# One load of x in place of two, on SP's queue and re-formed by VectorE, in a decode kernel

## The chip, the cores and the metric

The kernel runs on one core of one Trainium2 chip. The metric is the device time of one execution in microseconds (us). For the kernel before, three runs gave 407.74, 407.78 and 407.82 us; the median is 407.78. The profile is of one more execution, which took 407.74 us.

## The reference, cut to what matters

One token's x (1024 numbers) is normalised, then two blocks are computed from the normalised row and added to x: an attention block A over a cache of 65,536 positions with 4 key/value heads and 32 query heads, and a mixer/MLP block B.

```python
def _layernorm(x, axis=-1, eps=1e-5):
    m = jnp.mean(x, axis=axis, keepdims=True)
    v = jnp.var(x, axis=axis, keepdims=True)
    return (x - m) / jnp.sqrt(v + eps)

def _A_ref(x, k_cache, v_cache, wq, wo):
    q = (x @ wq) as 32 heads of 128
    scores = q . k * (128 ** -0.5)        # each key head serves 8 query heads
    o = softmax(scores) . v
    return o @ wo

def _B_ref(x, w1, w2, w3, w4):
    h = _gelu(_layernorm(x) @ w1)
    hs = (h, shifted along a sequence of length one, so zeros) @ w2
    x1 = x + hs
    return x1 + _gelu(_layernorm(x1) @ w3) @ w4

xn = _layernorm(A_x)
return A_x + _A_ref(xn, ...) + _B_ref(xn, ...)
```

All inputs are bfloat16. The cache is 2 x 64 MB, the weights together 35.7 MB, x is 2 KB.

## The kernel before, in words

**What is loaded.** One list, `order` (lines 585 to 598), names all large loads in the order in which they are used: four of wq, one of w1, one of w2, four of w3, then keys and values in turn, with wo in between and w4 last. Most are 2 MB, as 16 KB on each of 128 partitions (w3: 14 KB). All are issued by SP on its own DMA queue (`load`, line 276; q1 on the page) into nine slots of `slots_sb` that are used in rotation. `issue_to(NS - 1)` (line 614) issues the first nine; after the code of item i has been laid out, `issue_to(i + 9)` (line 641) issues the load that reuses its slot, and SP waits for the last reader of that slot first. w4's last two slots are loaded in pieces (`load_pieces`, line 284).

**How the order is made.** `_Q` collects each engine's instructions in program order, and `_op`, `_grp` and `_dma` add waits from what each tile was last written and read by (`_B`). An engine works through its list in order; a wait holds up all that is behind it on that engine. All waits of SP for its slots are at line 48.

**Constants.** GpSimd fills constants until about 8 us (lines 343 to 366), among them `ones_f` and the masks; `b_const` marks their end. TensorE's first three small matmuls (lines 374 to 376) wait for it.

**x.** It is loaded twice, by two DMAs that ACT issues (its queue is q10 on the page). `xP_bf` (line 368) is x on 128 partitions, 8 numbers each; `xr_bf` (line 370) is x as four rows of 256 numbers on partitions 0, 32, 64 and 96, into a tile that VectorE has set to zero (line 369). Both count on one semaphore, and the cast of `xP_bf` to float32 `xP` (line 372) waits for both.

**The norm and its users.** `layer_norm` (from line 391) reduces `xP` on VectorE, sums over partitions with a TensorE matmul against ones (lines 393 and 401), takes the power on GpSimd (line 405) and leaves `xn_bf`. Then VectorE makes `accr` from `xr_bf`, `ln_s` and `xr_bf` again (lines 601 and 603): x plus its normalised form in four rows, to which the results of all products are added at the end (line 642). `rows_mv` (line 411) multiplies a vector with a loaded slab: its matmuls (line 417) leave the result as four rows, one for each quarter of the columns. `use_wq` does so for wq, two slabs' rows at a time, into two PSUM banks.

**From rows to partitions.** `to_p` (line 420) brings such four rows to 128 partitions: one VectorE transpose of 32x32 blocks (line 421) into `X32[:, 1, ...]`, the second half of the tile that the key transposes also use, from which every 32nd column is then read. w1, w2, wq and w3 use it for their results.

**Attention.** For each key load VectorE makes four transposes (line 499) and TensorE multiplies (line 506); VectorE takes the maximum (line 511), ACT the exponential (line 530); TensorE transposes the weights (line 539) and multiplies with the value loads (line 552). `wo` and `w4` products follow at line 417, and SP stores the result (line 643).

Of the kernel before, what the change touches and what calls it, by code (L numbers as in the profile page):

```python
# [6 lines left out]
BF = mybir.dt.bfloat16  # L7
F32 = mybir.dt.float32
ACTF = mybir.ActivationFunctionType
ALU = mybir.AluOpType  # L10
# [64 lines left out]
def _deps(q, reads, writes):  # L75
    for b in reads:
        for s, v in b.w.items():
            q.wait((s, v))
    for b in writes:
        for s, v in b.w.items():  # L80
            q.wait((s, v))
        for s, v in b.r.items():
            q.wait((s, v))


def _done(ev, reads, writes, partial=False):
    for b in reads:
        b.add_read(ev)
    for b in writes:
        if partial:  # L90
            b.add_write(ev)
        else:
            b.set_write(ev)


def _op(q, fn, reads=(), writes=(), partial=False):
    _deps(q, reads, writes)
    ev = q.op(fn, True)
    _done(ev, reads, writes, partial)
    return ev  # L100
# [17 lines left out]
def _dma(q, chan, fn, reads=(), writes=(), partial=False):  # L118
    _deps(q, reads, writes)
    chan.n += 1  # L120
    ev = q.dma(fn, chan.sem, 16 * chan.n)
    _done(ev, reads, writes, partial)
    return ev
# [10 lines left out]
def bass_parallel_sum__gqa_block_cached__mixer_s_mlp__decode_kernel(  # L134
# [14 lines left out]
    P = 128  # L149
# [6 lines left out]
    R = D // P  # L156
# [10 lines left out]
    RW = D // 4  # L167
# [7 lines left out]
    with ExitStack() as es:  # L175
# [3 lines left out]
        def sb(name, shape, dt):  # L179
            return E(nc.sbuf_tensor(name, shape, dt))  # L180
# [4 lines left out]
        def sem(name):  # L185
            return E(nc.semaphore(name))
# [12 lines left out]
        neghalf = sb("neghalf", [P, 1], F32)  # L199
        permWE = sb("permWE", [P, 4, P], BF)  # L200
        maskA = sb("maskA", [P, 4, G], F32)
        xP_bf = sb("xP_bf", [P, R], BF)
        xP = sb("xP", [P, R], F32)
        xn = sb("xn", [P, R], F32)
        xn_bf = sb("xn_bf", [P, R + 32], BF)
# [5 lines left out]
        ln_s = sb("ln_s", [P, 8], F32)  # L211
# [21 lines left out]
        cb_o = sb("cb_o", [P, R], F32)  # L233
        oP_bf = sb("oP_bf", [P, HKV * R + 32], BF)
        xr_bf = sb("xr_bf", [P, RW], BF)
        accr = sb("accr", [P, RW], F32)
        g_bf = sb("g_bf", [P, R + 32], BF)
        ge_x = sb("ge_x", [P, NT], F32)
# [14 lines left out]
        q_dve = _Q("dve", sem("c_dve"))  # L253
        q_act = _Q("act", sem("c_act"))
        q_pool = _Q("pool", sem("c_pool"))
        q_sp = _Q("sp", None)
        ch_x = _DmaChan(sem("d_x"))
        ch_out = _DmaChan(sem("d_out"))
        slots = [_Slot(slots_sb[:, i, :], _B("slot%d" % i), _DmaChan(sem("d_s%d" % i))) for i in range(NS)]

        b_const = _B(); b_xb = _B(); b_x = _B(); b_xn = _B(); b_xn2 = _B(); b_x1 = _B(); b_xn3 = _B()
        b_ln = _B(); b_qT = _B(); b_Y = _B(); b_misc = _B(); b_ge = _B()
        b_X = [[_B() for _ in range(4)] for _ in range(2)]
        b_S = [_B() for _ in range(NCH)]
# [3 lines left out]
        b_Bst = _B(); b_brun = [_B(), _B()]; b_dd = _B(); b_ff = _B()  # L268
        b_p = _B(); b_pT = [_B(), _B()]; b_lcol = [_B(), _B()]; b_lsum = _B(); b_Lacc = _B(); b_O = _B()
        b_cb = _B(); b_oP = [_B() for _ in range(HKV)]  # L270
        b_xr = _B(); b_accr = _B(); b_h1 = _B(); b_gh = _B(); b_fin = _B()


        n_load = [0]
# [1 line left out]
        def load(src, width=SLOT):  # L276
            sl = slots[n_load[0] % NS]
            n_load[0] += 1
            view = sl.view[:, 0:width]
            _dma(q_sp, sl.chan, lambda e, view=view, src=src: e.dma_start(out=view, in_=src), writes=[sl.buf])  # L280
            return view, sl.buf
# [83 lines left out]
                                                          compare_op=ALU.not_equal, fill=1.0, base=-16 * j, channel_multiplier=1))  # L365
        b_const.set_write(ev)

        _dma(q_act, ch_x, lambda e: e.dma_start(out=xP_bf[:, :], in_=A_x[0, 0, :].rearrange("(p r) -> p r", p=P)), writes=[b_xb])
        _op(q_dve, lambda e: e.memset(xr_bf[:], 0.0), writes=[b_xr])
        _dma(q_act, ch_x, lambda e: e.dma_start(out=xr_bf[0:P:32, :], in_=A_x[0, 0, :].rearrange("(j m) -> j m", j=4)), writes=[b_xr])  # L370
        b_xb.add_write((ch_x.sem, 16 * ch_x.n))
        _op(q_dve, lambda e: e.tensor_copy(xP[:], xP_bf[:]), reads=[b_xb], writes=[b_x])

        _op(q_pe, lambda e: e.matmul(M1_ps[:, 0:P], selGT_bf[:, :], selGT_bf[:, :], start=True, stop=True), reads=[b_const], writes=[b_M1])
        _op(q_pe, lambda e: e.matmul(M1_ps[:, P:P + 8], selGT_bf[:, :], ident_bf[0:8, 0:8], start=True, stop=True), reads=[b_const], writes=[b_M1], partial=True)
# [13 lines left out]
        X32 = X[:].bitcast(F32)  # L389

        def layer_norm(src, b_src, dst_f, dst_bf, b_dst, c0):
            _op(q_dve, lambda e: e.reduce_sum(ln_s[:, 0:1], src[:], axis=AX.X), reads=[b_src], writes=[b_ln])
            _op(q_pe, lambda e: e.matmul(M0_ps[:, c0:c0 + 1], ones_f[:, :], ln_s[:, 0:1], start=True, stop=True),  # L393
                reads=[b_ln, b_const], writes=[b_M0])
            _op(q_dve, lambda e: e.tensor_scalar(out=ln_s[:, 1:2], in0=M0_ps[:, c0:c0 + 1], scalar1=-1.0 / D, scalar2=None, op0=ALU.mult),
                reads=[b_M0], writes=[b_ln])
            _op(q_dve, lambda e: e.tensor_scalar(out=ln_xc[:], in0=src[:], scalar1=ln_s[:, 1:2], scalar2=None, op0=ALU.add),
                reads=[b_src, b_ln], writes=[b_ln])
            _op(q_dve, lambda e: e.tensor_tensor(out=ln_sq[:], in0=ln_xc[:], in1=ln_xc[:], op=ALU.mult), reads=[b_ln], writes=[b_ln])
            _op(q_dve, lambda e: e.reduce_sum(ln_s[:, 2:3], ln_sq[:], axis=AX.X), reads=[b_ln], writes=[b_ln])  # L400
            _op(q_pe, lambda e: e.matmul(M0_ps[:, c0 + 1:c0 + 2], ones_f[:, :], ln_s[:, 2:3], start=True, stop=True),  # L401
                reads=[b_ln, b_const], writes=[b_M0])
            _op(q_dve, lambda e: e.tensor_scalar(out=ln_s[:, 3:4], in0=M0_ps[:, c0 + 1:c0 + 2], scalar1=1.0 / D, scalar2=EPS,
                                                 op0=ALU.mult, op1=ALU.add), reads=[b_M0], writes=[b_ln])
            _op(q_pool, lambda e: e.tensor_tensor(out=ln_s[:, 4:5], in0=ln_s[:, 3:4], in1=neghalf[:, 0:1], op=ALU.pow),
                reads=[b_ln, b_const], writes=[b_ln])
            _op(q_dve, lambda e: e.tensor_scalar(out=dst_f[:], in0=ln_xc[:], scalar1=ln_s[:, 4:5], scalar2=None, op0=ALU.mult),
                reads=[b_ln], writes=[b_dst])
            _op(q_dve, lambda e: e.tensor_copy(dst_bf[:, 0:R], dst_f[:]), reads=[b_dst, b_const], writes=[b_dst])
# [10 lines left out]
        def to_p(src, c0, n, b_src):  # L420
            _op(q_dve, lambda e: e.transpose(out=X32[:, 1, c0:c0 + 32 * n], in_=src), reads=b_src, writes=[b_X[1][0]], partial=c0 > 0)  # L421
# [168 lines left out]
        for n in range(NK):  # L590
# [6 lines left out]
        order.append(("wo", HKV - 1))  # L597
        order += [("w4", i) for i in range((F + 1023) // 1024)]

        layer_norm(xP, b_x, xn, xn_bf, b_xn, 0)  # L600
        _op(q_dve, lambda e: e.tensor_scalar(out=accr[:], in0=xr_bf[:], scalar1=ln_s[:, 1:2], scalar2=ln_s[:, 4:5], op0=ALU.add, op1=ALU.mult),
            reads=[b_xr, b_ln], writes=[b_accr])
        _op(q_dve, lambda e: e.tensor_tensor(out=accr[:], in0=accr[:], in1=xr_bf[:], op=ALU.add), reads=[b_xr, b_accr], writes=[b_accr])
        loaders = {"wq": load_wq, "w1": lambda: load(w1_v[:, 0:SLOT]), "w2": lambda: load(w2_v[:, 0:SLOT]), "w3": load_w3, "wo": load_wo, "w4": load_w4,
                   "k": load_k, "v": load_v}

        issued = []

        def issue_to(i):
            while len(issued) <= i and len(issued) < len(order):  # L610
                it = order[len(issued)]
                issued.append(loaders[it[0]](*it[1:]))

        issue_to(NS - 1)
        for i, it in enumerate(order):
            kind, args = it[0], it[1:]
            ld = issued[i]
            if kind == "wq":
                if args[0] == 3:
                    late_consts()  # L620
                    layer_norm(xn, b_xn, xn2, xn2_bf, b_xn2, 2)
                use_wq(args[0], ld)
            elif kind == "k":
                g, ch = args
                use_k(g, ch, ld)
                if ch == 0 and g > 0:
                    transpose_p(g - 1)
                if ch == NCH - 1:
                    finish_group(g)
            elif kind == "v":  # L630
                g, a = args
                if g == NG - 1 and a == 0:
                    transpose_p(g)
                use_v(g, a, ld)
                if a == NA - 1:
                    flash(g)
                    if g % GPH == GPH - 1:
                        combine(g // GPH)
            else:
                dict(w1=use_w1, w2=use_w2, w3=use_w3, wo=use_wo, w4=use_w4)[kind](*args, ld)  # L640
            issue_to(i + NS)
# [37 lines left out]
```

## Time and profile before

| | |
|---|---|
| runs of the kernel before, median (lowest to highest) | 407.78 us (407.74 to 407.82) |
| the profiled execution | 407.74 us |
| its span, from the first to the last instruction | 406.0 us |
| mean granted TensorE clock | 0.591 of full speed |
| busy: TensorE matmul, VectorE, ACT, GpSimd | 169.5, 201.0, 64.9, 7.5 us |
| SP's queue q1 | 169.88 MB in 12,536 packets, 98.7% of 16 DMA engines' span |
| ACT's queue q10 (the two loads of x) | 152 packets, 0.0% |
| instruction fetches (q8 and q14) | 18 packets, 0.25 MB |
| read from HBM | 169.87 MB, 418 GB/s over the span |

Times in the profile are in us from the span's start. Engines are PE (TensorE matmul), PEld (its weight load), DVE (VectorE), ACT, POOL (GpSimd) and SP; a "q" behind the name is the engine's sequencer, which issues DMAs. L499 is line 499 of the kernel. A row of the timeline has start, duration, engine, line, operation, the tile written, the tile read, shapes and a count; in brackets stands how long the engine was idle before and what ended that. A row of the windows has the stretch, its length, each engine's busy time with the number of instructions, the granted TensorE clock, the busy share of the 16 DMA engines and the GB/s that they moved. The chain of waits follows the work that ended last back to the start. The trace also keeps each DMA packet's queue, start, duration and size; a semaphore write is a packet of 4 bytes.

### The profile page before, as it was taken

Reading aid. Unit: us, or ns where it says so; the run is one execution under the profiler, and the core shown is the slowest. Engines: PE = TensorE matmul, PEld = TensorE weight load, DVE = VectorE, ACT = ScalarE, POOL = GpSimd, SP = SyncE. Lnnn points to the kernel's source line nnn. Section 1 sums busy time; section 2 is a strip of 40 time slices with the busy share of each in tenths; the row PEclk is TensorE's granted clock in tenths of the full one; section 3 lists DMA queues with packets and bytes.
Section 4 is the critical chain, followed back from the end, with each engine's and each line's share of the span. In section 5 each row is a group of like instructions: output and inputs, shape, how many; then the busy total and the mean of one; then the engine's idle time right before and its main releaser. Section 6 shows DMA issues by size and latency. Waiting matters only on the chain.

```text
span 406.0 us, 4087 instructions
## 1 busy us (share of the span) xinstructions
PE 169.5 (42%) x1651; PEld 72.2 (18%) x1651; DVE 201.0 (50%) x304; ACT 64.9 (16%) x91; POOL 7.5 (2%) x38
## 2 busy tenths in 40 slices
PE   0544313127437324641353354623533535433644
PEld 0222000003113102211121122211211312211221
DVE  0453066765775556554655547526545477160100
ACT  1000000042043005200520052003400421007000
POOL 5000000000000000000000000000000000000000
PEclk9955555555656665665555555665666556655856
DMA  8999999999999999999999999999999999999995
GB/s 335 431 423 430 422 433 425 429 434 420 429 426 428 433 425 429 426 423 431 426 425 429 423 429 433 423 431 425 429 428 428 428 426 428 424 433 428 426 413 198
DMA packets 12706, 170.14 MB, mean 419 GB/s; under 512 B 1544, under 2 KB 1552, under 8 KB 2448
## 3 DMA queue, kind: packets, MB, share of 16 engines
q1 hardware_dynamic: 12536, 169.88, 98.7%
q8 instruction: 13, 0.21, 0.2%
q14 instruction: 5, 0.04, 0.0%
q10 hardware_dynamic: 152, 0.00, 0.0%
HBM read 169.87 MB, written 0.00 MB: 418 GB/s over the span
## 4 chain that ended last, share of the span: by engine, by line
DMA 68%; DVE 13%; PE 9%; SPq 4%; issue 3%; ACT 1%; POOL 0%; ACTq 0%
DMA slots_sb<-in_A_k_cache_dram 50%; DVE X L499 11%; DMA slots_sb<-in_A_wo_dram 10%; DMA slots_sb<-in_B_w_dram 6%; PE S_ps L506 5%; SPq L293 4%; DMA xr_bf<-in_A_x_dram 2%; PE OT_ps L552 2%; DVE mcol L511 1%; ACT pT_sb L542 1%; PE PT_ps L539 1%; PE S_ps L417 1%; PE M_ps L417 0%; PE M_ps L401 0%; PE M_ps L393 0%
## 5 line engine op out<-in xcount | busy, mean ns | idle before, releaser
L499 DVE STREAM_TRANSPOSE X<-slots_sb 128x1024 f32<-128x1024 f32 x128 | 147.8, 1212 | 43.7 <-DMA slots_sb<-in_A_k_cache_dram 43.7
L506 PE MATMUL S_ps<-X,Yall 128*32 128x512 bf16 x512 | 60.6, 621 | 149.1 <-DVE X L499 139.4
L530 ACT ACTIVATE p_sb<-S_ps,brun 128x512 bf16<-128x512 f32 x32 | 44.9, 1403 | 215.6 <-DVE brun L522 110.5
L552 PE MATMUL OT_ps<-slots_sb,pT_sb 128*32 128x512 bf16 x512 | 54.7, 573 | 11.2 <-ACT pT_sb L542 9.6
L511 DVE TENSOR_REDUCE mcol<-S_ps 128x1 f32<-128x512 f32 x32 | 22.1, 692 | 69.3 <-PE S_ps L506 69.3
L506 PEld LDWEIGHTS S_ps<-X,Yall 128*32 128x32 bf16 x512 | 17.4, 128 | 185.1 <-DVE X L499 168.5
L552 PEld LDWEIGHTS OT_ps<-slots_sb,pT_sb 128*32 128x32 bf16 x512 | 18.4, 130 | 35.2 <-issue 31.8
L542 ACT ACTIVATE pT_sb<-PT_ps 128x1024 bf16<-128x1024 bf16 x16 | 16.4, 1023 | 41.0 <-PE PT_ps L539 41.0
L539 PE MATMUL PT_ps<-ident_bf,p_sb 128*128 128x128 bf16 x128 | 15.3, 294 | 13.5 <-ACT pT_sb L542 8.9
L417 PE MATMUL S_ps<-slots_sb,xn_bf 128*32 128x512 bf16 (+1 forms) x128 | 13.0, 559 | 13.3 <-DMA slots_sb<-in_B_w_dram 7.0
L539 PEld LDWEIGHTS PT_ps<-ident_bf,p_sb 128*128 128x128 bf16 x128 | 11.4, 132 | 22.3 <-ACT pT_sb L542 11.0
L421 DVE STREAM_TRANSPOSE X<-S_ps 128x512 f32<-128x512 f32 (+1 forms) x3 | 2.5, 850 | 16.7 <-PE S_ps L417 16.6
L417 PE MATMUL M_ps<-slots_sb,gh_bf 128*32 128x256 bf16 x112 | 7.0, 392 | 9.0 <-DMA slots_sb<-in_B_w_dram 8.9
L642 DVE TENSOR_TENSOR fin<-accr,M_ps 128x256 bf16<-128x256 f32 x1 | 0.4, 422 | 18.3 <-PE M_ps L417 18.3
L569 DVE TENSOR_TENSOR O_acc<-O_acc,OT_ps 128x512 f32<-128x512 f32 x4 | 2.8, 688 | 13.1 <-PE OT_ps L552 13.1
L429 ACT ACTIVATE ge_a<-ge_b 128x8 f32<-128x8 f32 (+1 forms) x2 | 0.4, 218 | 51.0 <-DVE ge_b L428 51.0
L417 PE MATMUL M_ps<-slots_sb,oP_bf 128*32 128x256 bf16 x128 | 5.9, 346 | 6.0 <-DMA slots_sb<-in_A_wo_dram 6.0
L530 ACT ACTIVATION_READ_ACCUMULATOR p_sb<-S_ps,brun 128x1 f32 x32 | 8.4, 261 | 0.0
L417 PEld LDWEIGHTS S_ps<-slots_sb,xn_bf 128*32 128x32 bf16 x128 | 4.0, 127 | 20.4 <-DMA slots_sb<-in_B_w_dram 10.9
L574 PE MATMUL M_ps<-O_acc,selX 128*128 128x128 f32 x32 | 7.3, 401 | 0.0
L574 PEld LDWEIGHTS M_ps<-O_acc,selX 128*128 128x128 f32 x32 | 6.5, 298 | 0.0
L520 PE MATMUL M_ps<-Rm,Lmat 128*128 128x16 bf16 x8 | 1.6, 196 | 9.6 <-DVE Rm L518 9.6
(97 smaller groups left out, 66.8 us busy)
## 6 DMA issues: line engine op xcount, KB each, us to landing
slots_sb<-in_A_k_cache_dram SPq DMA_DIRECT2D x32, 2048.0 KB, 39.4
slots_sb<-in_A_v_cache_dram SPq DMA_DIRECT2D x32, 2048.0 KB, 39.1
slots_sb<-in_A_wq_dram SPq DMA_DIRECT2D x4, 2048.0 KB, 14.0
slots_sb<-in_B_w_dram SPq DMA_DIRECT2D x4, 2048.0 KB, 34.8
slots_sb<-in_A_wo_dram SPq DMA_DIRECT2D x4, 2048.0 KB, 40.7
slots_sb<-in_B_w_dram SPq DMA_DIRECT2D x4, 1792.0 KB, 36.9
slots_sb<-in_B_w_dram SPq DMA_DIRECT2D x5, 512.0 KB, 35.8
slots_sb<-in_B_w_dram SPq DMA_DIRECT2D x2, 256.0 KB, 26.0
```

What stands on the lines that cost most here:

```text
L293: ev = q_sp.dma(lambda e, dst=dst, src=src: e.dma_start(out=dst, in_=src), ch.sem, 16 * ch.n)
L417: e.matmul(out_fn(j), st_fn(kk), mv_fn(kk, j), start=st, stop=sp, tile_position=(0, 32 * j), skip_group_check=True))
L421: _op(q_dve, lambda e: e.transpose(out=X32[:, 1, c0:c0 + 32 * n], in_=src), reads=b_src, writes=[b_X[1][0]], partial=c0 > 0)
L499: _op(q_dve, lambda e, ix=ix: e.transpose(out=X32[:, m, 1024 * ix:1024 * (ix + 1)], in_=K32[:, 1024 * ix:1024 * (ix + 1)]), reads=[b], wri ...
L506: fns.append(lambda e, we=we, c_mid=c_mid, mv=mv: e.matmul(S_ps[ch][32 * c_mid:32 * c_mid + 32, :], Yall[:, h, we, :, :].rearrange("p a g ...
L511: _op(q_dve, lambda e: e.reduce_max(mcol[:, gm, ch:ch + 1], S_ps[ch][:, :], axis=AX.X), reads=[b_S[ch]], writes=[b_mcol[gm]], partial=ch > 0)
L530: _op(q_act, lambda e, ch=ch: e.activation(p_sb[:, :, :, ch], S_ps[ch][:, :].rearrange("p (c i) -> p c i", i=32), ACTF.Exp, bias=brun[:, k ...
L539: _grp(q_pe, [lambda e, i=i, c=8 * c8 + i: e.transpose(out=PT_ps[:, i * P:(i + 1) * P], in_=p_sb[:, c, :, :].rearrange("p i h -> p (i h)") ...
L542: _op(q_act, lambda e, c8=c8, m=m: e.activation(pT_sb[:, m, :, 32 * c8:32 * c8 + 32, :].rearrange("p a x g -> p x a g"), PT_ps[:, :].rearr ...
L552: fns.append(lambda e, cl=cl, q4=q4: e.matmul(OT_ps[32 * q4:32 * q4 + 32, :], pT_sb[:, m, a, 4 * cl:4 * cl + 4, :].rearrange("p x g -> p ( ...
L569: _op(q_dve, lambda e: e.tensor_tensor(out=O_acc[:, :], in0=O_acc[:, :], in1=OT_ps[:, :], op=ALU.add), reads=[b_OT], writes=[b_O])
L574: fns.append(lambda e, t=t: e.matmul(M0_ps[:, 256:384], selX[:, t, :, :].rearrange("p g x -> p (g x)"), O_acc[:, t * P:(t + 1) * P], start ...
```

## The change

x is loaded once, by a DMA that SP issues after the first load of wq, as four rows into `xr_bf`. The DMA into `xP_bf` and that tile are gone, and ACT issues no DMA any more. VectorE casts `xr_bf` to a new float32 tile `xr` of the same four rows, transposes that with `to_p` and copies every 32nd column of the result into `xP`. The norm starts from `xP` as before. The two operations that make `accr` read `xr` instead of `xr_bf`. These instructions, the norm's first call among them, stand behind the calls that issue the first nine loads in the program, where they stood ahead of them; SP, which issues, and VectorE have lists of their own.

```diff
-        xP_bf = sb("xP_bf", [P, R], BF)
...
         xr_bf = sb("xr_bf", [P, RW], BF)
+        xr = sb("xr", [P, RW], F32)
...
-        _dma(q_act, ch_x, lambda e: e.dma_start(out=xP_bf[:, :], in_=A_x[0, 0, :].rearrange("(p r) -> p r", p=P)), writes=[b_xb])
         _op(q_dve, lambda e: e.memset(xr_bf[:], 0.0), writes=[b_xr])
-        _dma(q_act, ch_x, lambda e: e.dma_start(out=xr_bf[0:P:32, :], in_=A_x[0, 0, :].rearrange("(j m) -> j m", j=4)), writes=[b_xr])
-        b_xb.add_write((ch_x.sem, 16 * ch_x.n))
-        _op(q_dve, lambda e: e.tensor_copy(xP[:], xP_bf[:]), reads=[b_xb], writes=[b_x])
+
+        def load_x():
+            _dma(q_sp, ch_x, lambda e: e.dma_start(out=xr_bf[0:P:32, :], in_=A_x[0, 0, :].rearrange("(j m) -> j m", j=4)), writes=[b_xr])
...
-        layer_norm(xP, b_x, xn, xn_bf, b_xn, 0)
-        _op(q_dve, lambda e: e.tensor_scalar(out=accr[:], in0=xr_bf[:], scalar1=ln_s[:, 1:2], scalar2=ln_s[:, 4:5], op0=ALU.add, op1=ALU.mult),
-            reads=[b_xr, b_ln], writes=[b_accr])
-        _op(q_dve, lambda e: e.tensor_tensor(out=accr[:], in0=accr[:], in1=xr_bf[:], op=ALU.add), reads=[b_xr, b_accr], writes=[b_accr])
...
+        issued = []
+        issue_to(0)
+        load_x()
         issue_to(NS - 1)
+        _op(q_dve, lambda e: e.tensor_copy(xr[:], xr_bf[:]), reads=[b_xr], writes=[b_xr32])
+        to_p(xr[:, :].rearrange("p (c r) -> p r c", r=R), 0, R, [b_xr32])
+        _op(q_dve, lambda e: e.tensor_copy(xP[:], X32[:, 1, 0:32 * R:32]), reads=[b_X[1][0]], writes=[b_x])
+        layer_norm(xP, b_x, xn, xn_bf, b_xn, 0)
+        _op(q_dve, lambda e: e.tensor_scalar(out=accr[:], in0=xr[:], scalar1=ln_s[:, 1:2], scalar2=ln_s[:, 4:5], op0=ALU.add, op1=ALU.mult),
+            reads=[b_xr32, b_ln], writes=[b_accr])
+        _op(q_dve, lambda e: e.tensor_tensor(out=accr[:], in0=accr[:], in1=xr[:], op=ALU.add), reads=[b_xr32, b_accr], writes=[b_accr])
```

More of the change, by code (lines that the diff above doesn't have):

```diff
@@ L259, in bass_parallel_sum__gqa_block_cached__mixer_s_mlp__decode_kernel @@
         slots = [_Slot(slots_sb[:, i, :], _B("slot%d" % i), _DmaChan(sem("d_s%d" % i))) for i in range(NS)]
-        b_const = _B(); b_xb = _B(); b_x = _B(); b_xn = _B(); b_xn2 = _B(); b_x1 = _B(); b_xn3 = _B()
+        b_const = _B(); b_x = _B(); b_xn = _B(); b_xn2 = _B(); b_x1 = _B(); b_xn3 = _B()
         b_ln = _B(); b_qT = _B(); b_Y = _B(); b_misc = _B(); b_ge = _B()
@@ L270, in bass_parallel_sum__gqa_block_cached__mixer_s_mlp__decode_kernel @@
         b_cb = _B(); b_oP = [_B() for _ in range(HKV)]
-        b_xr = _B(); b_accr = _B(); b_h1 = _B(); b_gh = _B(); b_fin = _B()
+        b_xr = _B(); b_xr32 = _B(); b_accr = _B(); b_h1 = _B(); b_gh = _B(); b_fin = _B()
         n_load = [0]
@@ L598, in bass_parallel_sum__gqa_block_cached__mixer_s_mlp__decode_kernel @@
         order += [("w4", i) for i in range((F + 1023) // 1024)]
-        layer_norm(xP, b_x, xn, xn_bf, b_xn, 0)
-        _op(q_dve, lambda e: e.tensor_scalar(out=accr[:], in0=xr_bf[:], scalar1=ln_s[:, 1:2], scalar2=ln_s[:, 4:5], op0=ALU.add, op1=ALU.mult),
-            reads=[b_xr, b_ln], writes=[b_accr])
-        _op(q_dve, lambda e: e.tensor_tensor(out=accr[:], in0=accr[:], in1=xr_bf[:], op=ALU.add), reads=[b_xr, b_accr], writes=[b_accr])
         loaders = {"wq": load_wq, "w1": lambda: load(w1_v[:, 0:SLOT]), "w2": lambda: load(w2_v[:, 0:SLOT]), "w3": load_w3, "wo": load_wo, "w4": load_w4,
                    "k": load_k, "v": load_v}
-        issued = []
         def issue_to(i):
```

## The prediction

> **What bounds the kernel now.** I read the page's busy lines and queue lines first, then the 20-us windows, then the chain of waits, then the timeline of the first 20 us.
>
> ```profile
> span 406.0 us, 4087 instructions
> ...
> q1 hardware_dynamic: 12536, 169.88, 98.7%
> q8 instruction: 13, 0.21, 0.2%
> q14 instruction: 5, 0.04, 0.0%
> q10 hardware_dynamic: 152, 0.00, 0.0%
> ```
>
> q1 is SP's queue, with all weights and the cache; q10 is ACT's, with the two copies of x. No compute engine is busy for more than half of the span, but q1 keeps the 16 DMA engines busy 98.7% of it. The windows (last two columns: DMA share, GB/s) say the same stage by stage:
>
> ```profile
> 4.00:24.00 20.00, 7.87 (x71) 4.07 (x75) 5.61 (x27) 0.00 (x0) 3.82 (x14) 0.89 1.01 432
> 24.00:44.00 20.00, 9.19 (x112) 4.42 (x104) 8.11 (x36) 0.21 (x1) 0.55 (x1) 0.50 0.99 420
> ...
> 364.00:384.00 20.00, 10.68 (x107) 5.33 (x107) 2.23 (x9) 8.10 (x12) 0.00 (x0) 0.65 1.01 428
> 384.00:404.00 20.00, 8.93 (x145) 4.39 (x144) 1.49 (x5) 0.00 (x0) 0.00 (x0) 0.60 0.85 347
> ```
>
> The share is 0.99 to 1.02 in every window between 4 and 384 us: there is no gap in the stream that an earlier or later x could close or open. The trace's packet records (queue, start, duration, size of each) give its ends: the first q1 packet starts at 1.81 us, the last ends at 402.56. So the span is 1.81 + 400.75 of stream + 3.44 of tail (last matmuls, the final add, the output's DMA) = 406.0; the profiled execution took 407.74, so 1.74 lie outside the span. It is 0.04 under the median, 407.78.
>
> The chain of waits begins with x, and this is the trap of the page:
>
> ```profile
> 1.25 8.08 DMA xr_bf<-in_A_x_dram
> ...
> 13.31 3.31 PE S_ps L417 x31
> ...
> 16.69 39.26 DMA slots_sb<-in_A_k_cache_dram
> ```
>
> From x it goes through the first layer norm and the first wq matmuls into the issue of a k load at 16.69, which lands 39.26 us later. That load did not need 39 us: it stood behind seven others, and eight loads at 4.3 to 4.9 us each make the 39. An issue that comes a microsecond earlier lands at the same time.
>
> **The change, part by part.**
>
> The two DMAs on ACT go. In q10 the packet records show 128 packets of 16 bytes for xP_bf, 4 of 512 bytes for xr_bf, and 20 semaphore writes, interleaved with q1's from 2.95 to 9.0 us. All 152 last 1.42 us together, 0.09 us for each of the 16 engines. The 144 that go without replacement (128 packets and their 16 semaphore writes) are the gain of the stream: at least 0; at most some 0.2 if the start is eased too (q1's issue and ACT's stand side by side at 0.79 and 0.80 us, and two engines take their first packet 0.3 and 0.6 us after the others). I take 0.05, since the first eight rounds of q1 packets passed at 0.616 us each with those packets between them and the next eight at 0.609: 7 or 8 times 0.007.
>
> The one DMA on SP stands between wq's first and second load. Its cost on SP is an issue. The rows:
>
> ```profile
> 0.79 2.03 SPq L280 DMA_DIRECT2D slots_sb<-in_A_wq_dram  x4
> 0.80 0.41 ACTq L368 DMA_DIRECT2D xP_bf<-in_A_x_dram  x1
> 0.88 0.17 DVE L369 MEMSET xr_bf<- 128x128 uint32 x1 [0.88 <-PEq L664]
> 1.25 1.07 ACTq L370 DMA_DIRECT2D xr_bf<-in_A_x_dram  x1
> ...
> 403.95 0.65 SPq L643 DMA_DIRECT2D out_dram<-fin  x1
> ```
>
> The same four rows took ACT 1.07 us to issue, and SP 0.65 for the output's four rows, so wq's second load is issued at 2.0 to 2.4 us instead of 1.3. Its first packet is due when the first load's last has gone, at 7.3 to 7.7 us: some 5 us of cover, cost nothing. The new wait on SP is for the memset of xr_bf, done at 1.05 us while SP still issues the first load (0.79 + 2.03/4 = 1.30); every later load is queued behind that wait, with the same 5 us of cover. In the queue, x puts one 512-byte packet (27 ns) and one semaphore write (9 ns) on four engines, as it did in q10: nothing net.
>
> The way to the first matmul. Now x lands late because its 9 packets per engine take turns with q1's, one each: the rows move at 8.08 to 8.36, their semaphore writes come at 8.71 to 8.99, VectorE starts at 9.35. Behind the first load they move at some 7.4 to 7.7 with the semaphore write next, and 0.36 us on (8.99 to 9.35), VectorE starts at about 8.1. Bounds: 7.8 (nothing late) to 9.35 (nothing gained). VectorE then has a cast of 128x256, a transpose and a pick of every 32nd column, where it had one small cast (0.17, L372). Cast: between the 0.17 of that row and the 0.41 of L601 (256 columns from bf16, with arithmetic); 0.29 by the slope from 8 columns (0.17) to 128 (0.23, L383). Transpose: 0.44, the row L421 of the same shape, from PSUM; not under 0.30, a quarter of L499's 1.21. Pick: 0.17 (L425). With gaps of 0.03 the norm's first reduction starts at 8.1 + 0.29 + 0.44 + 0.17 + 0.1 = 9.1 us instead of 9.56: 0.45 earlier (bounds: 0.85 earlier to 0.75 later). The norm itself is unchanged, so the first matmul moves from 13.31 to about 12.85. What is late next:
>
> ```profile
> 13.31 3.29 PE L417 MATMUL S_ps<-slots_sb,xn_bf 128*32 128x512 bf16 x32 [1.45 <-DVE xn_bf L409]
> ...
> 17.95 1.05 PE L417 MATMUL S_ps<-slots_sb,xn_bf 128*32 128x512 bf16 x16 [1.35 <-DMA slots_sb<-in_A_wq_dram]
> ```
>
> PE finishes two loads of wq at 16.60 and waits 1.35 us for the third. An earlier x makes that wait longer, a later one (0.75) is still swallowed by it. So the 0.45 us ends there, and the gain is nothing. The slots that come free earlier let SP issue earlier into a queue that is some 30 us deep (the ninth load's last packets move at 44.6 to 46.3 us, the tenth is issued by 15.6).
>
> The two operations for accr read float32 (0.41 and 0.42 us now; I bound each by 0.2 to 0.6, the spread of 128x128 float32 rows, 0.23 and 0.31, carried to 256 columns). They stand behind xn_bf, VectorE is idle again from 16.16 on, and accr is needed at 403.5: nothing, up to the 3 us before wq's third load.
>
> Sum: 1.81 + (400.75 - 0.05) + 3.44 + 1.74 = 407.69, so **407.7 us**.
>
> **A cost that the diff does not name: addresses.** xP_bf is declared ahead of the slots. Tiles start at multiples of 32 bytes in the built program, and slots_sb stands at byte 23,616, a multiple of 64 and 64 past one of 256. Without xP_bf all that follows, up to xr, moves down by 32 bytes, and slots_sb to 23,584. If the address counts, it counts in each of the roughly 640 large q1 packets per engine. At the measured pace (16,384 bytes in 0.612 us) 32 bytes are 1.2 ns, so a packet that needs one step of 32 bytes more or less moves the stream by 640 x 1.2 ns = 0.8 us, one of 64 bytes by 1.6. The nearest row is xr_bf's own: it stands 32 past a multiple of 64, and its 512-byte packets take 27 ns, 8 over the 19 that this pace makes; the 2,048-byte packets of w4 in the aligned slots take 84, also 8 over their 76. That row shows no penalty at such an address, so I take 0 and keep -0.8 and +1.6.
>
> **Rivals.**
>
> *Slower by the address (0.13).* Place: every q1 packet. Price: +0.8 to +1.6 us, 408.5 to 409.3. It decides if a 16 KB packet takes over 0.613 us in the first steady window. For it: nothing else touches all packets. Against: the xr_bf row.
>
> *Faster by the address (0.08).* If a packet also pays for the bytes between the 256-byte boundary below its start and the start, it pays for 64 bytes now and 32 after: -0.8 us, 406.9. Against: xr_bf starts 96 past such a boundary and its packets show no more fixed time than those of the slots. The Trainium skill, DMA: Bandwidth & Descriptors, section "How a descriptor splits into AXI transactions", states that rule for what a descriptor fetches: the bytes below an unaligned start cost beats too. By that rule, applied to the written side, the sum would be 406.9; by the row, 407.7; the row is of this chip and I follow it.
>
> *The slowest engine changes (0.08).* The 16 engines do not end together: the last load's semaphore writes are spread from 401.12 to 402.56, because single engines also fetch instructions (q8, q14; 16 KB each taking 1.0 to 1.1 us). A fetch that falls on another engine costs up to 1.0 us, or gives back some 0.3 if it leaves the slowest: 407.4 to 408.7, half of it slower by over 0.8. Against: VectorE and SP gain a few instructions, ACT loses a few, PE, with nearly all fetches, none.
>
> *The change doesn't do what it says (x lands no earlier, or later, within the nothing-changes case).* Whether x comes at 8.1 or 10 us, the third load of wq decides at 17.95: 407.7 as well. It would take a delay of tens of microseconds to drain the queue.
>
> **Chances and range.** Nothing that can be told apart: 0.71 (407.3 to 408.0). The address, slower: 0.13; faster: 0.08. The engines: 0.08, half of it slower, half within. A measurement of this kernel tells about 0.2%, 0.8 us, from no change; an address gain of 0.8 would stand at that edge and I count it as faster. That makes faster 0.08, same 0.71 + 0.04 = 0.75, slower 0.13 + 0.04 = 0.17. Range: 406.9 to 408.7, which takes in the gain by address and the smaller of the two losses.
>
> **What would show it.** Right: q10 gone from the queue lines; xr_bf's landing near 8.1 us and the first reduction near 9.1; the third load of wq still awaited until 17.9 to 18.0 with PE idle about 1.8 us before it; windows of 420 to 432 GB/s as now; the last q1 packet at 402.5. Wrong: another landing time of the later loads of wq, windows that differ all along by 0.2% or more (address), or a last packet that moves while the windows don't (engines).

## The result, and the profile after

The changed kernel takes 408.40 us (median of 20 runs, 408.30 to 408.52) where the kernel before takes 407.82 (20 runs, 407.71 to 408.00): the ratio is 1.0014, with a 95% interval of 1.0008 to 1.0021. It is slower, by less than the 0.2% that the prediction called no change, but clearly so: the interval leaves out 1. The profiled execution of the changed kernel took 408.41 us.

The page of the changed kernel, its span and its queue lines:

```profile
span 406.7 us, 4088 instructions
...
q1 hardware_dynamic: 12544, 169.88, 98.7%
q8 instruction: 13, 0.21, 0.2%
q14 instruction: 5, 0.04, 0.0%
```

q10 is gone, q1 has the eight packets of x more, and the instruction fetches are as many as before. The span is 0.7 us longer. The timeline of the changed kernel shows that this does not come from the part that the diff rewrites:

```profile
0.78 0.39 SPq L280 DMA_DIRECT2D slots_sb<-in_A_wq_dram  x1
1.24 0.69 SPq L371 DMA_DIRECT2D xr_bf<-in_A_x_dram  x1
1.97 1.49 SPq L280 DMA_DIRECT2D slots_sb<-in_A_wq_dram  x3
...
8.07 0.29 DVE L612 CAST xr<-xr_bf 128x256 f32<-128x256 bf16 x1 [7.02 <-DMA xr_bf<-in_A_x_dram]
8.40 0.64 DVE L420 STREAM_TRANSPOSE X<-xr 128x256 f32<-128x256 f32 x1
9.07 0.17 DVE L614 COPY xP<-X 128x8 f32<-128x8 f32 x1
9.28 0.16 DVE L391 TENSOR_REDUCE ln_s<-xP 128x1 f32<-128x8 f32 x1
...
13.04 3.61 PE L416 MATMUL S_ps<-slots_sb,xn_bf 128*32 128x512 bf16 x32 [1.46 <-DVE xn_bf L408]
...
17.83 1.90 PE L416 MATMUL S_ps<-slots_sb,xn_bf 128*32 128x512 bf16 x16 [1.19 <-DMA slots_sb<-in_A_wq_dram]
```

VectorE has x at 8.07 us, the norm begins at 9.28 instead of 9.56, the first matmul at 13.04 instead of 13.31, and the third load of wq is awaited as before. Up to here the changed kernel is ahead, not behind. The loss is in the rest of the stream. These are the packets that start between 45 and 385 us, by the DMA view: first the kernel before, then the changed one.

```profile
DMA packets 9996, 145.38 MB, mean 428 GB/s; under 512 B 1106, under 2 KB 1106, under 8 KB 1106
```

```profile
DMA packets 9976, 145.10 MB, mean 427 GB/s; under 512 B 1103, under 2 KB 1103, under 8 KB 1103
```

In the same 340 us, 0.28 MB less were moved; at 428 GB/s that is 0.65 us. The packet records say how: a 16 KB packet takes 615.6 ns on average before and 616.5 after (half of them 613 ns before and 614 after, a fifth 620 and 621). With some 640 large packets on each of the 16 engines, 0.86 ns each makes 0.55 us. The last packet of the loads ends at 403.27 us instead of 402.56, and the tail behind it is as long as it was: 3.4 us.

### The profile page after: what moved, and what is told of

Read it like the earlier page. It is cut to its first block, busy times and chain, and to the rows that moved or that the text cites. A ratio compares the mean times of both kernels' runs of the same rounds, so it can differ in the third digit from the quotient of the medians.

```text
span 406.7 us, 4088 instructions
## 1 busy us (share of the span) xinstructions
PE 176.6 (43%) x1651; PEld 75.3 (19%) x1651; DVE 202.0 (50%) x306; ACT 65.0 (16%) x91; POOL 7.6 (2%) x38
## 4 chain that ended last, share of the span: by engine, by line
DMA 66%; DVE 14%; PE 11%; SPq 4%; issue 3%; ACT 1%; POOL 0%
DMA slots_sb<-in_A_k_cache_dram 48%; DVE X L498 11%; DMA slots_sb<-in_A_wo_dram 10%; DMA slots_sb<-in_B_w_dram 6%; PE S_ps L505 5%; SPq L293 4%; PE OT_ps L551 2%; DMA xr_bf<-in_A_x_dram 2%; DVE mcol L510 1%; ACT pT_sb L541 1%; PE PT_ps L538 1%; PE S_ps L416 1%; PE M_ps L416 1%; PE M_ps L573 0%; DVE O_acc L568 0%
## 5 line engine op out<-in xcount | busy, mean ns | idle before, releaser
L551 PE MATMUL OT_ps<-slots_sb,pT_sb 128*32 128x512 bf16 x512 | 57.3, 597 | 10.6 <-ACT pT_sb L541 9.6
L541 ACT ACTIVATE pT_sb<-PT_ps 128x1024 bf16<-128x1024 bf16 x16 | 16.4, 1024 | 41.8 <-PE PT_ps L538 41.8
L416 PE MATMUL S_ps<-slots_sb,xn_bf 128*32 128x512 bf16 (+1 forms) x128 | 14.1, 601 | 12.0 <-DMA slots_sb<-in_B_w_dram 6.9
L416 PE MATMUL M_ps<-slots_sb,oP_bf 128*32 128x256 bf16 x128 | 6.8, 381 | 5.6 <-DMA slots_sb<-in_A_wo_dram 4.2
L573 PE MATMUL M_ps<-O_acc,selX 128*128 128x128 f32 x32 | 8.2, 439 | 0.0
L416 PEld LDWEIGHTS M_ps<-slots_sb,oP_bf 128*32 128x32 bf16 x128 | 4.3, 129 | 9.3 <-DMA slots_sb<-in_A_wo_dram 8.5
```

The costliest lines, as they stand in the source:

```text
L416: e.matmul(out_fn(j), st_fn(kk), mv_fn(kk, j), start=st, stop=sp, tile_position=(0, 32 * j), skip_group_check=True))
L541: _op(q_act, lambda e, c8=c8, m=m: e.activation(pT_sb[:, m, :, 32 * c8:32 * c8 + 32, :].rearrange("p a x g -> p x a g"), PT_ps[:, :].rearr ...
L551: fns.append(lambda e, cl=cl, q4=q4: e.matmul(OT_ps[32 * q4:32 * q4 + 32, :], pT_sb[:, m, a, 4 * cl:4 * cl + 4, :].rearrange("p x g -> p ( ...
L573: fns.append(lambda e, t=t: e.matmul(M0_ps[:, 256:384], selX[:, t, :, :].rearrange("p g x -> p (g x)"), O_acc[:, t * P:(t + 1) * P], start ...
```

## The experiments

What the load of x touches directly could not reach every packet until 400 us. Three causes were left: the tiles' addresses (all behind `xP_bf`, up to `xr`, stand 32 bytes lower); the queue, that is, another phase of the DMA engines against each other after another start; and instruction fetches that fall on other engines.

**The old addresses under the changed kernel.** An unused tile stands where `xP_bf` stood; its 16 bytes move all that follows by 32.

```diff
+        xP_bf = sb("xP_bf", [P, R], BF)
         xP = sb("xP", [P, R], F32)
```

> The changed kernel, with an unused 16-byte tile declared where xP_bf stood, so that slots_sb and all behind it, up to xr, keep the addresses of the kernel before (slots_sb at a multiple of 64 bytes, not 32 past one). Theory A (addresses: each large packet of SP's queue takes 614 ns instead of 613 in the middle of the run because the slots moved by 32 bytes): the packets return to 613 ns, the last one ends near 402.6 us, and the time is 407.7 to 407.9 us. Rival B (queue and phase: the DMA engines step differently against each other because ACT's small packets are gone and x stands in SP's queue): 614 ns stay, 408.3 to 408.5 us. Rival C (instruction fetches falling on other engines): the packets are as in the kernel before but the last one ends at 403.0 or later, 408.2 or more.

Measured: 407.75 us, ratio to the kernel before 0.9997 (0.9988 to 1.0006). The DMA view between 45 and 385 us:

```profile
DMA packets 9996, 145.40 MB, mean 428 GB/s; under 512 B 1105, under 2 KB 1105, under 8 KB 1105
```

The 0.28 MB are back, the packets take 615.6 ns again, and the last one ends at 402.57. The whole loss goes away with one unused tile.

**The new addresses under the kernel before.** `xP_bf` is declared last.

```diff
-        xP_bf = sb("xP_bf", [P, R], BF)
...
         fin = sb("fin", [P, RW], BF)
+        xP_bf = sb("xP_bf", [P, R], BF)
```

> The kernel before, with xP_bf declared last instead of ahead of the slots: the addresses of the changed kernel and nothing else of it. Theory A (addresses): 614 ns packets and 408.3 to 408.5 us. Rival B (queue and phase): 613 ns and 407.7 to 407.9 us. Rival C (instruction fetches): the same instructions as before, so 407.7 to 407.9 us.

Measured: 408.57 us, ratio 1.0018 (1.0009 to 1.0027). The same view:

```profile
DMA packets 9979, 145.12 MB, mean 427 GB/s; under 512 B 1105, under 2 KB 1105, under 8 KB 1105
```

Two loads of x on ACT, no transpose, the instructions of the kernel before, and the changed kernel's loss: addresses alone make it.

**Both loads of x on SP's queue, old addresses; and the one load of x on ACT's queue, new addresses.** The first moves the two DMAs of the kernel before, and the norm with them, behind the first load of wq; the second turns one word of the changed kernel. (The lines that move away, and the ends of long lines, are left out and marked by dots.)

```diff
...
+        issue_to(0)
+        _dma(q_sp, ch_x, lambda e: e.dma_start(out=xP_bf[:, :], ...), writes=[b_xb])
+        _dma(q_sp, ch_x, lambda e: e.dma_start(out=xr_bf[0:P:32, :], ...), writes=[b_xr])
...
         issue_to(NS - 1)
...
```

> The kernel before at its own addresses, with both loads of x moved from ACT's queue to SP's, behind the first load of wq; no transpose, no new tile. Theory A (addresses): 407.7 to 407.9 us, 613 ns packets. Rival B (queue and phase): 408.2 to 408.5 us, 614 ns.

```diff
-            _dma(q_sp, ch_x, lambda e: e.dma_start(out=xr_bf[0:P:32, :], ...
+            _dma(q_act, ch_x, lambda e: e.dma_start(out=xr_bf[0:P:32, :], ...
```

> The changed kernel at its own addresses, with its one load of x issued by ACT on ACT's queue instead of by SP. Theory A (addresses): 614 ns packets and 408.3 to 408.5 us. Rival B (queue and phase): between the two kernels, since the four rows are back in ACT's queue but the 128 small packets are not: 407.7 to 408.2 us. Either way the norm starts within 1 us of where it starts in the changed kernel, and this does not show in the time.

Measured, in this order: 407.88 us (ratio 1.0000, 0.9992 to 1.0009) and 408.51 us (1.0016, 1.0007 to 1.0025). The queue of x does not matter, the addresses do; the rival of queue and phase is out. The second run also tells what an earlier norm is worth. Its timeline:

```profile
8.05 0.16 DVE L391 TENSOR_REDUCE ln_s<-xP 128x1 f32<-128x8 f32 x1
...
11.81 3.61 PE L416 MATMUL S_ps<-slots_sb,xn_bf 128*32 128x512 bf16 x32 [1.46 <-DVE xn_bf L408]
```

The norm begins 1.23 us earlier than in the changed kernel, more than the 1 us that I had allowed for, and the time is that of the other kernels at these addresses.

**Which tile, and what in the address.** Four variants of the changed kernel with unused tiles ahead of the slots (and in one of them behind). The remarks behind # are not in the kernels.

```diff
+        pad_a = sb("pad_a", [P, 240], BF)     # 480 bytes: slots at a multiple of 512
         slots_sb = sb("slots_sb", [P, NS, SLOT], BF)
```

> The changed kernel with an unused tile ahead of slots_sb, so that the slots start at a multiple of 512 bytes (480 further up). Three theories of what in the address counts. A1 (only whether a packet's first byte stands at a multiple of 64, so that no 64-byte unit is half used): 613 ns in steady state, 407.7 to 407.9 us. A2 (how far below the start the last 256-byte boundary lies, the fewer bytes the better): best of all, 407.0 or less. A3 (how far above the start the next 256-byte boundary lies): as bad as the changed kernel or worse, 408.4 to 409.5 us, or, if a start right at the boundary costs nothing, below 407.0.

```diff
+        pad_a = sb("pad_a", [P, 16], BF)      # 32 bytes: slots as in the kernel before
         slots_sb = sb("slots_sb", [P, NS, SLOT], BF)
+        pad_b = sb("pad_b", [P, 16], BF)      # the next tiles 32 past a multiple of 64
```

> The changed kernel with only slots_sb at its old address, a multiple of 64; the tile for the transposed keys and most tiles behind it stay 32 past a multiple of 64, by a second unused tile behind the slots. If the slots' address alone counts (what the loads write): 407.7 to 407.9 us. If it is the tile for the transposed keys or another one behind it: 408.3 to 408.5 us.

```diff
+        pad_a = sb("pad_a", [P, 32], BF)      # 64 bytes: slots 96 past a multiple of 256
         slots_sb = sb("slots_sb", [P, NS, SLOT], BF)
```

> As the run with only the slots at their old address, all tiles behind the slots at the same addresses as there, but the slots 32 bytes further up: 32 past a multiple of 64 and 96 past one of 256. A1 (multiple of 64): 408.3 to 408.5 us. A2 (distance from the 256-byte boundary below): worse than the changed kernel, some 409.5 us or more. A3 (distance to the 256-byte boundary above): better than the kernel before, 407.2 us or less.

```diff
+        pad_a = sb("pad_a", [P, 48], BF)      # 96 bytes: slots 128 past a multiple of 256
         slots_sb = sb("slots_sb", [P, NS, SLOT], BF)
```

> The changed kernel with the slots at a multiple of 128 bytes that is no multiple of 256 (96 further up). A1 (multiple of 64): 407.7 to 407.9 us. A2 (distance from the boundary below): 410 us or more. A3 (distance to the boundary above): 406.8 us or less.

The DMA view between 45 and 385 us, one kernel each: slots at a multiple of 512; slots alone old; at 96; at 128.

```profile
DMA packets 10061, 146.36 MB, mean 430 GB/s; under 512 B 1112, under 2 KB 1112, under 8 KB 1112
```

```profile
DMA packets 9995, 145.39 MB, mean 428 GB/s; under 512 B 1105, under 2 KB 1105, under 8 KB 1105
```

```profile
DMA packets 9996, 145.41 MB, mean 428 GB/s; under 512 B 1105, under 2 KB 1105, under 8 KB 1105
```

```profile
DMA packets 9991, 145.35 MB, mean 428 GB/s; under 512 B 1103, under 2 KB 1103, under 8 KB 1103
```

Measured: 404.98, 407.86, 407.75 and 407.69 us. The second and the third are both back at the time before, with the tile of the transposed keys 32 past a multiple of 64 in both: a multiple of 64 is needed neither for that tile nor for the slots. So A1, my first theory, falls with the third: 96 is no multiple of 64, and costs nothing over 64. A2 and A3 fall with the third and the fourth: at 96 A2 had 409.5 us or more and A3 407.2 or less, at 128 A2 had 410 or more and A3 406.8 or less.

The times alone do not part the slots from the tile of the transposed keys, since in all kernels but the second both stand equally far past a multiple of 256, and in the second the one stands at 64, the other at 96. The packet records do. With the slots at 64 and that tile at 96 (the second), 52% of the 16 KB packets take 613 ns and 21% take 620, as in the kernel before (52 and 20%); with both at 96 (the third), it is 15% and 4%, and the commonest time is 612. The packets' times follow the slots, into which they write.

And the first opened what I had not looked for: at a multiple of 512 the kernel is 2.9 us faster than the kernel before (ratio 0.9928, 0.9915 to 0.9942).

**The last three** ask where the cut is, whether it has two sides, and whether x has a part in the gain.

```diff
# the kernel before
+        pad_a = sb("pad_a", [P, 224], BF)     # 448 bytes: slots at a multiple of 512
```

> The kernel before, with an unused tile ahead of slots_sb so that the slots start at a multiple of 512 bytes; x is loaded as before, twice, by ACT. If the gain of the aligned slots (2.9 us in the changed kernel) has nothing to do with the change of x: 404.8 to 405.2 us and 611 ns packets in steady state. If part of it came from the way x is loaded: 405.5 us or more.

```diff
# the changed kernel
+        pad_a = sb("pad_a", [P, 112], BF)     # 224 bytes: slots at a multiple of 256, not of 512
```

> The changed kernel with the slots at a multiple of 256 bytes that is no multiple of 512. Theory T1 (a write is cut at every 256 bytes; a start between two cuts makes one piece more): 404.8 to 405.2 us, 611 ns. Theory T2 (the cuts are at every 512 bytes or further apart): 407.5 to 408.0 us.

```diff
# the changed kernel
+        pad_a = sb("pad_a", [P, 96], BF)      # 192 bytes: slots 224 past a multiple of 256
```

> The changed kernel with the slots 224 past a multiple of 256, so that a row's first piece up to the cut is 32 bytes and its last 224, the mirror of the changed kernel's 224 and 32. If only the smaller of the two pieces counts: 408.3 to 408.5 us, as in the changed kernel. If it is the last piece, and the more of it the better (32: 408.4, 64: 407.8, 96 and 128: 407.7): 407.5 to 407.7 us.

The same view of the three:

```profile
DMA packets 10064, 146.39 MB, mean 431 GB/s; under 512 B 1113, under 2 KB 1113, under 8 KB 1113
```

```profile
DMA packets 10064, 146.39 MB, mean 431 GB/s; under 512 B 1113, under 2 KB 1113, under 8 KB 1113
```

```profile
DMA packets 9975, 145.11 MB, mean 427 GB/s; under 512 B 1102, under 2 KB 1102, under 8 KB 1102
```

Measured: 404.87 us (ratio 0.9928, 0.9915 to 0.9942), 404.77 us (0.9925, 0.9912 to 0.9937) and 408.51 us (1.0015, 1.0006 to 1.0024). A multiple of 256 is enough, as T1 had it; 224 is as bad as 32, so the smaller piece counts; and the aligned kernel before gains as much as the aligned changed one. All thirteen kernels in one table, by what the slots stand past a multiple of 256:

| slots past a multiple of 256 | bytes to the nearer multiple | mean 16 KB packet, 45 to 385 us | kernels and times |
|---|---|---|---|
| 0 | 0 | 611.8 ns | 404.98, 404.87, 404.77 us |
| 128 | 128 | 615.5 ns | 407.69 us |
| 96 | 96 | 615.4 ns | 407.75 us |
| 64 (before) | 64 | 615.6 ns | 407.82, 407.75, 407.88, 407.86 us |
| 32 (after) | 32 | 616.5 ns | 408.40, 408.57, 408.51 us |
| 224 | 32 | 616.5 ns | 408.51 us |

A row of 16,384 bytes that does not start at a multiple of 256 crosses one multiple more, with a piece at either end. The table agrees with a price for that extra piece (some 3.7 ns a packet) and a little more when one end is as short as 32 bytes (0.9 ns). That the write is really cut there is argued from the pattern, not shown. In the three kernels of the first row the tile of the transposed keys stands at a multiple of 256 too; no run moves it away from there.

## Why the prediction was wrong, point by point

*The stream bounds the kernel.* Right: the times in the table go with those of the packets. 0.86 ns by 640 packets is 0.55 us, and the medians differ by 0.58. For the aligned slots 3.8 ns by 640 packets is 2.4 us of the 2.9; the rest is not accounted for here.

*SP's issue and its cover.* Right: x took 0.69 us to issue (0.65 to 1.07 forecast), the second load of wq was issued at 1.97 (2.0 to 2.4), and the third load of wq was awaited until 17.83, a little earlier than before.

*The way to the first matmul.* x at 8.07 (8.1), the cast 0.29 (0.29), the pick 0.17 (0.17). The transpose took 0.64 us where I took 0.44 from the same shape out of PSUM: out of SBUF, with the same strided view, it is slower, and I had bounded it from below only. So the norm came 0.28 us earlier and not 0.45. (The bounds of 0.85 earlier and 0.75 later are also narrower than their terms add up to, some 1.0 and 0.9; the 0.28 lies within both.) It cost nothing either way, as the run with x on ACT shows.

*The gain of 0.05 us in the stream.* Not seen and not refuted: at equal addresses the change makes 0.9997 (0.9988 to 1.0006) and 1.0000 (0.9991 to 1.0008). The reason given for it does not hold: counted in groups of 16 by their start, the second to ninth rounds of large packets follow each other at 0.623 us before and still at 0.619 after, and the next eight at 0.608 in both. The first rounds are slower without the 144 packets too.

*The addresses.* **This is the step that failed**: "That row shows no penalty at such an address, so I take 0". The term measured 0.58 us (408.40 against 407.82), 0.9 ns for each large packet. The row was xr_bf's, 512-byte packets that move at 8 us. At that time an address costs nothing: between 8 and 22 us the 16 KB packets take 611 ns in the kernel before, in the changed one and with the slots aligned alike. The DMA view between 8 and 22 us, before and after:

```profile
DMA packets 410, 6.03 MB, mean 431 GB/s; under 512 B 38, under 2 KB 42, under 8 KB 42
```

```profile
DMA packets 403, 6.03 MB, mean 431 GB/s; under 512 B 35, under 2 KB 35, under 8 KB 35
```

Equal bytes in equal time. The longer packets set in only between 21 and 29 us, by run, and then stay; with the slots at a multiple of 256 they do not: 99.7% of the packets between 45 and 385 us still take 611 ns. xr_bf's packets could not have told: by the sizes of the tiles it stands 96 past a multiple of 256 before, 64 after and exactly at one in the run with the slots at 224, and they take 27 ns in all three. Nor was w4's row a control: it moves at 398 to 402 us, but its slots stand 64 past a multiple of 256. 84 ns is the commonest of its times there, for half of the packets, and the mean is 85.8; with the slots at a multiple of 256 all 256 packets take 84. A row from the first 20 us can't price what an address costs in the 380 us behind it, and two unaligned rows can't show what alignment is worth.

*The rival that came true* had the place right (every large packet of q1), the sign, and the mark to look for (over 613 ns: the commonest time is 614). Its price, 0.8 to 1.6 us, was too high: the loss is 0.58. Its condition was wrong: not a multiple of 64, as the 96 shows, but the distance to a multiple of 256 on the nearer side. That its sign came true is luck so far: 32 bytes down also brought the slots nearer to a multiple of 256.

*The faster rival by the address* was wrong in sign. The Trainium skill, DMA: Bandwidth & Descriptors, section "How a descriptor splits into AXI transactions", puts the cuts at 256 bytes, and for the written side the runs here agree: 256 is enough (404.77 us). That the cost grows with the bytes below the start, which the section says of what is fetched, they do not bear out for what is written: 128 (407.69) costs no more than 64 (407.82), and 32 costs more (408.40). The measurement decides.

*The engines' ends.* Not the cause: with the changed kernel's instructions and the old addresses the last packet ended at 402.57.

## What to carry to other kernels

When a kernel is bound by its loads, a declaration is an edit like any other: before pricing a diff, list which tiles move, and look at where the destination of the large loads comes to stand. Place that destination at a multiple of 256 bytes: here an unused tile gives 0.7%, five times what the change of x lost, and the kernel before so padded (404.87 us) beats both kernels. To price a small cost that every packet pays, take packets of the same size from the stretch in which most of them move, and hold them against a row that is known not to pay it.

## What the runs showed of the hardware that was not expected

The rate of the loads depends on the start address of the row in each partition: 16 KB packets take 611.8 ns on average at multiples of 256 bytes and 615.4 to 616.5 at the five other offsets that were run, and 32 and 224 past the multiple are alike. The dependence sets in only after some 20 us of back-to-back loads; between 8 and 21 us nearly every 16 KB packet takes 611 ns, whatever the address. It is not a matter of wq, which is all that is loaded up to there: in the run with only the slots at their old address the packets of w1 take 611 ns too, until 27 us. Why it sets in is open; no run looked into it. And the VectorE transpose of 128x256 float32 took 0.64 us out of SBUF through a strided view, 0.44 out of PSUM through the same one; straight rows out of SBUF cost 1.21 us for 1,024 columns, 0.30 for 256 by that pace, so it is the view out of SBUF that is dear.
